# Turning the third to fifth pairs' q and k by the DMA crossbar instead of TensorE, with one more matmul on zeros

## The chip, the cores and the metric

The kernel runs on one core of a Trainium2 chip. The metric is the device time of one execution in microseconds, on an otherwise idle chip. "Half clock" and "full clock" below are TensorE's two rates. Pairs are counted from one: the "third pair" is `i == 2` in the code. The prediction counts from zero at places: its "pair 2" is the third pair here, its "pair 3" the fourth, its "pair 4" the fifth. A pair has nine units; in each, TensorE makes scores, ScalarE takes their exponential ("exp") and TensorE multiplies with the values. The "ring" is the line of transfers that SyncE has issued; GpSimd's transfers, w1 and w2 (the MLP's weights) among them, stand in another queue. The profile counts both on the same 16 DMA engines.

## The reference, cut to what matters

Block-sparse attention (a window, global blocks and sampled blocks of 32) over 4 batches of 8 heads, 768 positions, 64 wide, followed by a low-rank mixer and a two-layer MLP. Two heads make a pair; there are 16 pairs.

```python
scores = scale * np.matmul(q, k.transpose(0, 1, 3, 2))
scores = np.where(mask, scores, -1000000000.0)
attn = softmax(scores); out = np.matmul(attn, v)
x = out reshaped to (4, 768, 512)
u = x + (x^T @ U @ V)^T
result = u + relu(u @ w_ch1) @ w_ch2
```

(The last four lines are condensed.) q and k have a spread of 0.1, so scores are tiny.

## The kernel before

The scores need q and k with the head dimension on the partitions, so each pair is turned. The first four pairs run alone, before the MLP starts: they write q and k into the upper or lower 64 rows of tiles `qa` and `ka`, whose other 64 rows hold the mask as extra columns of the dot product. From the fifth pair (`HP` = 4) on the turned q and k stand in plain tiles `qT` and `kT`, and the mask is multiplied in by VectorE.

Before the change the second to fifth pairs are turned by TensorE into PSUM, and VectorE copies the result out. From the sixth on SyncE issues DMA transposes, SBUF to SBUF.

```python
def turn_dma(i, nm):
    st = sts.pop((i, nm))
    qkT[i, nm] = qkpool.tile([P, T, P], FP16, ...)
    keep(nc.sync.dma_start_transpose(out=qkT[i, nm], in_=st...))

def turn_part(i, nm, part):              # half a turn: 3 transposes
    ...
    turn_some(sts[i, nm], turning[nm], 3 * part, 3 * part + 3)
    if part == 1:
        ...
        if i < HP:
            for h in range(2):
                half_copy(nc.vector.tensor_copy, dst, h, pt, 0, T)
        else:
            keep(nc.vector.tensor_copy(out=qkT[i, nm], in_=pt))

def at_unit(i, u):                       # pair i, unit u of 9
    if (i, u) in MASKS:                  # (1, 8), (2, 8), (3, 8) among them
        mask_tiles(...)                  # two matmuls into PSUM, VectorE turns them into 0/1
    ...
    if u == 0 and i < 3:
        issue(i + 3)                     # SyncE: loads of q, k, v
    ...
    if (i, u) in WLOADS:                 # (1, 3), (1, 4), (2, 3), (2, 4): w1, by GpSimd
        WLOADS[i, u]()
    if u in (1, 2, 3, 4):
        turn_part(i + 1, "qk"[(u - 1) // 2], (u - 1) % 2)
    for _ in range({0: 1, 5: 2, 6: 1, 7: 1}.get(u, 0)):
        tails.popleft()()                # the mixer: at u = 6 and 7 the additions `xf`
    if u == 7: cast(i + 2, "q")          # GpSimd
    if u == 8: cast(i + 2, "k")
```

(Cuts at the dots.) The argument rests on VectorE's order. In the changed kernel's trace VectorE takes the copies and the additions `xf` in program order: the first addition, whose input was long there, starts only at 33.58 us, behind two copies that waited for a DMA until 32.82.

The softmax here doesn't subtract the row's maximum and nothing guards it: scores larger than these inputs give would overflow.

Of the kernel before, what the change touches and what calls it, by code (L numbers as in the profile page):

```python
# [21 lines left out]
def kernel(  # L22
# [12 lines left out]
    nc = tc.nc  # L35
# [6 lines left out]
    HP = H // 2  # L42
# [54 lines left out]
    keep = tc.keep_in_program_order  # L97
    flat = "p t n -> p (t n)"
# [10 lines left out]
    def pst_tile(shape, dtype, name, tag):  # L109
        n = singles[tag][0]  # L110
        singles[tag].rotate(1)
        return psp[tag].tile(shape, dtype, tag=f"{tag}{n}", name=name)
# [54 lines left out]
    def run_on(eng, us, ready=None):  # L167
        clk[eng] = max(clk[eng], (clk["pe"] if ready is None else ready) + LAG) + us
        return clk[eng]

    def mm(out, lhsT, rhs, start, stop, loose=False, us=0.0):
        clk["pe"] += us
        ins = nc.tensor.matmul(  # L173
            out, lhsT, rhs, start=start, stop=stop, skip_group_check=loose
        )
        keep(ins)
        return ins
# [16 lines left out]
    qa = [[consts.tile([P, S], FP16, name=f"qa{s}{h}") for h in range(2)] for s in range(2)]  # L194
    ka = [[consts.tile([P, S], FP16, name=f"ka{s}{h}") for h in range(2)] for s in range(2)]
# [15 lines left out]
    rows = [slice(0, D), slice(D, P)]  # L211
# [3 lines left out]
    lds, sts, qkT = {}, {}, {}  # L215
# [12 lines left out]
    def issue(i, names="qkv"):  # L228
        if i >= NPAIR:
            return  # L230
        for nm in names:
            keep(nc.sync.dma_start(out=new_ld(i, nm), in_=src_of(nm, i)))
# [30 lines left out]
    def turn_some(st, pt, t0, t1):  # L263
        for t in range(t0, t1):
            keep(
                nc.tensor.transpose(  # L266
                    out=pt[:, t, :],
                    in_=st[:, t].rearrange("p h d -> p (h d)"),
                    identity=id16,
                )  # L270
            )

    def turn_dma(i, nm):
        if i >= NPAIR:
            return
        st = sts.pop((i, nm))
        qkT[i, nm] = qkpool.tile([P, T, P], FP16, tag=nm + "T", name=nm + "T")
        keep(
            nc.sync.dma_start_transpose(
                out=qkT[i, nm], in_=st.rearrange("p t h d -> p (t h d)")  # L280
            )
        )
# [6 lines left out]
    for r in (slice(32, 64), rows[1]):  # L289
# [3 lines left out]
            out=id16, in_=zeros, pattern=[[-1, P]], compare_op=ALU.not_equal,  # L293
# [9 lines left out]
    def hot_rows(eng, st, h, n):  # L303
# [5 lines left out]
            out=sbi[0:NB].rearrange("z r w -> z (r w)"),  # L309
            in_=sampled_blocks.bitcast(I32),  # L310
# [28 lines left out]
    def warm_pe(n):  # L339
        for _ in range(n):  # L340
            mm(
                warm.rearrange("p (r n) -> p r n", r=4), zeros,
                zeros[:, None, :].broadcast_to([P, 4, P]), True, True,
            )
# [5 lines left out]
            out=eq[0:NB],  # L350
# [7 lines left out]
            out=cb[0:NB],  # L358
            in_=eq[0:NB].rearrange("z r c -> z c r"),
# [6 lines left out]
            out=cbd[0:NB, :, 0:NB],  # L366
# [16 lines left out]
    def mask_rows(eng, h, i, a, e):  # L383
        o = qa[0][h][mrows[h], a:e]
        if eng == "dve":
            keep(
                nc.vector.tensor_scalar(
                    out=o, in0=i[mrows[h]],
                    scalar1=-MASK_BIAS, scalar2=MASK_BIAS, op0=ALU.mult, op1=ALU.add,
                )  # L390
            )
        else:
            keep(
                nc.scalar.activation(
                    out=o, in_=i[mrows[h]],
                    func=AF.Copy, scale=-MASK_BIAS, bias=MASK_BIAS,
                )
            )
# [6 lines left out]
    cast0(nc.vector.tensor_copy, qst, qld, 0, TQ)  # L405
    mask_rows("dve", 0, pm0[:, 0, 0:QA], 0, QA)
    mask_rows("act", 1, pm1, 0, QA)
    pq = pst_tile([P, T, P], FP16, "pturn", tag="ps")
    pk = pst_tile([P, T, P], FP16, "pturn", tag="ps")
    turn_some(qst, pq, 0, TQ)  # L410
# [4 lines left out]
    def half_copy(eng, dst, h, pt, t0, t1):  # L415
        keep(
            eng(
                out=dst[h][rows[h], t0 * P : t1 * P],
                in_=pt[rows[h], t0:t1].rearrange(flat),
            )  # L420
        )
# [30 lines left out]
    def mask_tiles(g):  # L452

        pmk = [pst_tile([P, HS], FP32, "pmk", tag="ps") for c in range(2)]
        for c in range(2):
            mm(pmk[c], ka[0][c][mrows[c], g * P : (g + 1) * P],
               qa[0][c][mrows[c], c * HS : (c + 1) * HS], True, True)
        for c in range(2):
            keep(
                nc.vector.tensor_scalar(  # L460
                    out=m01[:, g, c * HS : (c + 1) * HS], in0=pmk[c],
                    scalar1=-1.0, scalar2=None, op0=ALU.is_ge,
                )
            )
# [470 lines left out]
    def turn_part(i, nm, part):  # L935

        if part == 0:
            turning[nm] = pst_tile([P, T, P], FP16, "pturn", tag="ps")
        turn_some(sts[i, nm], turning[nm], 3 * part, 3 * part + 3)
        if part == 1:  # L940
            del sts[i, nm]
            pt = turning.pop(nm)
            if i < HP:
                dst = {"q": qa, "k": ka}[nm][i % 2]
# [3 lines that stand above are left out]
                qkT[i, nm] = qkpool.tile([P, T, P], FP16, tag=nm + "T", name=nm + "T")  # L948
                keep(nc.vector.tensor_copy(out=qkT[i, nm], in_=pt))
            run_on("dve", 0.48)  # L950
# [25 lines left out]
    def cast_V():  # L976
        keep(
            nc.gpsimd.tensor_copy(
                out=Vt[0 : 2 * R, :, :],
                in_=mvld.rearrange("r (p t) -> r t p", t=T),  # L980
            )
        )

    def at_unit(i, u):
        if (i, u) in MASKS:
            mask_tiles(MASKS.index((i, u)))
        if i == 0:
            if u == 0:
                warm_pe(1)
                turn_some(qst, pq, TQ, T)  # L990
                turn_some(kst, pk, TK, T)
                for h in range(2):
                    mask_rows("dve", h, pm2[:, 0, 0:QB], QA, S)
                for nm, o, pt, t in (("q", qa[0], pq, TQ), ("k", ka[0], pk, TK)):
                    for h in range(2):
                        half_copy(nc.vector.tensor_copy, o, h, pt, t, T)
                for h in range(2):
                    keep(
                        nc.sync.dma_start(
                            out=qa[1][h][mrows[h], :], in_=qa[0][h][mrows[h], :]  # L1000
                        )
                    )
                issue(2, "q")
                keep(
                    nc.sync.dma_start(
                        out=uld, in_=moe_U.rearrange("(p t) r -> p (t r)", t=T)
                    )
                )
                issue(2, "k")
                for h in range(2):  # L1010
                    keep(nc.sync.dma_start(out=mvld[h * R : h * R + R], in_=moe_V))
                cast(1, "q")
                cast(1, "k")
                cast(1, "v")
            if u == 1:
                issue(2, "v")
            if u == 3:
                issue(3)
            if u == 6:
                cast(2, "q")  # L1020
                cast_U()
                cast(2, "k")
            if u == 4:
                turn_part(1, "q", 0)
                turn_part(1, "q", 1)
            if u == 6:
                turn_part(1, "k", 0)
                turn_part(1, "k", 1)
            return
        if u == 0 and i < 3:  # L1030
            issue(i + 3)
        if i == 1 and u == 2:
            cast_V()
            cast(2, "v")
        if i == 2 and u == 0:
            for h in range(2):
                keep(nc.sync.dma_start(out=Vd[rows[h]], in_=Vt[rows[0]]))
        if (i, u) in WLOADS:
            WLOADS[i, u]()
        if u in (1, 2, 3, 4):  # L1040
            turn_part(i + 1, "qk"[(u - 1) // 2], (u - 1) % 2)
        for _ in range({0: 1, 5: 2, 6: 1, 7: 1}.get(u, 0)):
            if tails:
                tails.popleft()()
        if u == 7:
            cast(i + 2, "q")
        if u == 8:
            cast(i + 2, "k")
        if u == 0 and i > 1:
            cast(i + 1, "v")  # L1050
# [211 lines left out]
```

## Time and profile before

| | before |
|---|---|
| median of the runs beside the changed kernel | 278.41 us (278.13 to 279.15, 4 runs) |
| profiled span | 277.7 us |
| TensorE, ScalarE, VectorE busy | 98%, 64%, 63% |
| chain of waits: TensorE | 92% |
| first exp of pairs 1 to 5 | 8.22, 17.36, 25.77, 34.28, 43.03 us |

These lines of the page cut the span into 40 slices of 6.9 us; each digit is an engine's busy share in tenths. The last line is the chain of waits by engine.

```profile
PE   7999999999999999999999999999999999999995
ACT  3799996786977957694864849584886201664000
DMA  6997965998969998997790999997100312000222
...
PE 92%; ACT 3%; DVE 2%; DMA 1%; POOL 0%; issue 0%; SPq 0%; DVEq 0%; POOLq 0%
```

TensorE hardly ever stops. In slices 2 to 6, most of the first four pairs, ScalarE (7, then 9s) and the DMA engines (9, 9, 7, 9, 6) are nearly full as well.

### The profile page before, as it was taken

What the parts mean: (1) busy time and instruction counts of PE and PEld (TensorE: products, weight loads), DVE (VectorE), ACT (ScalarE), POOL (GpSimd) and SP (SyncE); (2) the same over time, 40 slices, a digit from 0 to 9 for tenths busy, and PEclk for the clock granted to TensorE, in tenths of its full rate; (3) what the DMA queues carried; (4) which work ended last, traced back from release to release, by engine and by line L of the source; (5) the groups of instructions that cost most, each with busy time, mean ns of one, the idle gap of its engine ahead of it and who ended that gap; (6) DMA issues with size and microseconds to landing.
All of it is one profiled execution on the core that took longest, in us unless ns stands there. A gap on an engine that the chain in (4) does not pass through costs nothing.

```text
span 277.7 us, 8035 instructions
## 1 busy us (share of the span) xinstructions
PE 271.5 (98%) x3492; PEld 162.6 (59%) x3492; DVE 175.3 (63%) x286; ACT 177.0 (64%) x198; POOL 103.5 (37%) x137
## 2 busy tenths in 40 slices
PE   7999999999999999999999999999999999999995
PEld 2568775566656564756565564656565654655443
DVE  6767767888897987767756768776777451000112
ACT  3799996786977957694864849584886201664000
POOL 5659549506465736363603536361102020000000
PEclk9999999999999999999999999999999999999999
DMA  6997965998969998997790999997100312000222
GB/s 204 312 326 195 282 155 79 176 187 81 135 56 110 171 135 129 162 102 81 57 118 0 173 95 163 135 97 86 31 2 2 104 68 81 36 1 0 78 77 76
DMA packets 85484, 31.65 MB, mean 114 GB/s; under 512 B 75152, under 2 KB 83048, under 8 KB 85448
## 3 DMA queue, kind: packets, MB, share of 16 engines
q0 software_dynamic: 49824, 10.29, 43.4%
q1 hardware_dynamic: 35268, 20.62, 34.3%
q8 instruction: 27, 0.44, 0.7%
q10 hardware_dynamic: 356, 0.22, 0.3%
q14 instruction: 9, 0.07, 0.1%
HBM read 27.84 MB, written 6.29 MB: 123 GB/s over the span
## 4 chain that ended last, share of the span: by engine, by line
PE 92%; ACT 3%; DVE 2%; DMA 1%; POOL 0%; issue 0%; SPq 0%; DVEq 0%; POOLq 0%
PE pch L173 30%; PE pt L173 30%; PE psc L173 13%; PE pav L173 13%; ACT est L498 3%; PE pa L173 2%; DMA qld<-in_q_dram 1%; PE pturn L266 1%; PE ph L173 1%; POOL xh L598 0%; PE warm L173 0%; PE puT L711 0%; DVE xh L541 0%; PE pmk L173 0%; DVE xs L589 0%
## 5 line engine op out<-in xcount | busy, mean ns | idle before, releaser
L498 ACT ACTIVATE est<-psc 128x1024 f16<-128x1024 f32 x144 | 142.9, 1028 | 46.1 <-PE psc L173 44.7
L173 PE MATMUL pt<-uT,w1t 64*128 64x384 f16 (+1 forms) x896 | 94.4, 324 | 0.0
L173 PE MATMUL pch<-w2t,tT 64*128 64x512 f16 (+3 forms) x688 | 93.6, 372 | 0.1
L519 DVE TENSOR_TENSOR est<-est,m 128x1024 f16<-128x1024 f16 x108 | 78.3, 740 | 18.2 <-ACT est L498 16.8
L173 PEld LDWEIGHTS <-w1t 64*128 64x128 f16 (+1 forms) x896 | 46.0, 95 | 36.2 <-PE pt L173 8.3
L173 PEld LDWEIGHTS <-tT 64*128 64x128 f16 (+1 forms) x688 | 38.2, 95 | 36.9 <-PE pch L173 1.6
L736 ACT ACTIVATE tT<-pt 128x768 f16<-128x768 f32 (+1 forms) x48 | 36.6, 772 | 26.0 <-PE pt L173 26.0
L173 PEld LDWEIGHTS <-est 128*128 128x128 f16 x1152 | 41.4, 97 | 10.9 <-issue 5.0
L173 PE MATMUL pav<-vt,est 128*128 128x65 f16 x1152 | 44.5, 193 | 0.1
L791 DVE TENSOR_TENSOR of<-xf,pch 128x1024 f32<-128x1024 f32 (+3 forms) x16 | 15.2, 951 | 42.7 <-PE pch L173 42.7
L173 PE MATMUL psc<-qT,kT 64*128 64x512 f16 (+1 forms) x288 | 40.6, 323 | 0.3 <-ACT est L498 0.3
L598 POOL CAST xh<-xs 128x768 f16<-128x768 f32 x12 | 10.5, 872 | 79.6 <-DVE xs L589 74.0
L684 POOL CAST uh<-xf 128x768 f16<-128x768 f32 x12 | 13.9, 1162 | 26.1 <-DVE xf L675 14.5
L173 PE MATMUL psc<-qa,ka 128*128 128x512 f16 (+1 forms) x96 | 22.0, 333 | 0.6 <-ACT est L498 0.5
L738 DVE TENSOR_SCALAR tT<-pt 128x768 f16<-128x768 f32 (+1 forms) x20 | 18.3, 917 | 5.9 <-PE pt L173 5.8
L173 PEld LDWEIGHTS <-kT 64*128 64x128 f16 x288 | 14.6, 94 | 12.5 <-issue 0.7
L261 POOL DMA_DIRECT2D vt<-in_v_dram x20 | 16.4, 822 | 3.4 <-DMA w2t<-in_moe_w_ch_dram 3.4
L261 POOL DMA_DIRECT2D qst<-in_q_dram x20 | 16.3, 821 | 0.1
L261 POOL DMA_DIRECT2D kst<-in_k_dram x20 | 16.3, 822 | 0.0
L589 DVE TENSOR_TENSOR xs<-pav,rcp 128x768 f32<-128x768 f32 x12 | 11.5, 958 | 1.2
L675 DVE TENSOR_TENSOR xf<-xs,ph 128x768 f32<-128x768 f32 x12 | 11.4, 951 | 1.2 <-PE ph L173 1.2
L173 PEld LDWEIGHTS <-ka 128*128 128x128 f16 (+1 forms) x108 | 9.0, 99 | 3.7 <-issue 1.8
(70 smaller groups left out, 132.2 us busy)
## 6 DMA issues: line engine op xcount, KB each, us to landing
out_dram<-of SPq DMA_DIRECT2D x9, 512.0 KB, 3.3
vld<-in_v_dram SPq DMA_DIRECT2D x6, 384.0 KB, 6.5
w1t<-in_moe_w_ch_dram POOLq DMA_DIRECT2D x4, 512.0 KB, 9.1
w2t<-in_moe_w_ch_dram POOLq DMA_DIRECT2D x4, 512.0 KB, 10.1
qld<-in_q_dram SPq DMA_DIRECT2D x5, 384.0 KB, 5.5
kld<-in_k_dram SPq DMA_DIRECT2D x5, 384.0 KB, 6.8
qst<-in_q_dram POOLq DMA_DIRECT2D x20, 96.0 KB, 4.1
kst<-in_k_dram POOLq DMA_DIRECT2D x20, 96.0 KB, 4.4
```

The source lines that it names most:

```text
L173: ins = nc.tensor.matmul(out, lhsT, rhs, start=start, stop=stop, skip_group_check=loose)
L261: keep(nc.gpsimd.dma_start(out=o[:, h], in_=src_of(nm, i)[:, h]))
L266: nc.tensor.transpose(out=pt[:, t, :], in_=st[:, t].rearrange("p h d -> p (h d)"), identity=id16,)
L498: keep(nc.scalar.activation(out=est, in_=psc, func=AF.Exp, scale=0.125))
L519: keep(nc.vector.tensor_tensor(out=o, in0=o, in1=m, op=ALU.mult))
L589: nc.vector.tensor_tensor(out=xs.rearrange("p (c j) (h d) -> p c (j h) d", c=2, h=2), in0=pv[:, :, :, 0:D], in1=rcp[:, :, :, None].broadca ...
L598: keep(nc.gpsimd.tensor_copy(out=xh, in_=xs))
L675: nc.vector.tensor_tensor(out=u.rearrange("p (c j) n -> p c j n", c=2), in0=xs.rearrange("p (c j) n -> p c j n", c=2), in1=ph[:, :, 0:HS]. ...
L684: keep(nc.gpsimd.tensor_copy(out=uh, in_=u))
L736: keep(nc.scalar.activation(out=o, in_=i, func=AF.Relu))
L738: keep(nc.vector.tensor_scalar_max(out=o, in0=i, scalar1=0.0))
L791: nc.vector.tensor_add(out=of, in0=xfs[b][:, sc : sc + nsc, n0:n1], in1=pch)
```

## The change

The intent is to take 36 transposes off TensorE, the engine that carries the chain, and to put them on the DMA crossbar. The third and fourth pairs still need their rows inside `qa` and `ka`, so VectorE copies them there, SBUF to SBUF. The fifth pair's tiles are filled straight by the crossbar. One more matmul on zeros at the start is to keep TensorE busy while it waits for q.

```diff
     mask_rows("act", 1, pm1, 0, QA)
+    warm_pe(1)
     pq = pst_tile([P, T, P], FP16, "pturn", tag="ps")
...
-        if u in (1, 2, 3, 4):
-            turn_part(i + 1, "qk"[(u - 1) // 2], (u - 1) % 2)
+        if u == 0:
+            turn_dma(i + 1, "q")
+            turn_dma(i + 1, "k")
+        if u in (6, 7) and i + 1 < HP:
+            nm = "qk"[u - 6]
+            for h in range(2):
+                keep(
+                    nc.vector.tensor_copy(
+                        out={"q": qa, "k": ka}[nm][(i + 1) % 2][h][rows[h], :],
+                        in_=qkT[i + 1, nm][rows[h]].rearrange(flat),
+                    )
+                )
```

## The prediction

> **What bounds the kernel now.** I read the page's chain of waits first (TensorE 92% of it), then the slices, and then split the run at the point where its character changes. About 50 to 278 us TensorE works without a gap (tenths of busy all 9). Each engine's instruction order for that stretch, compared between the two kernels, is the same apart from the turns. So only the first four pairs (8 to 43 us) are in play. The stretches of that part:
>
> ```profile
> core 0: us, PE busy (x) PEld busy (x) DVE busy (x) ACT busy (x) POOL busy (x), PEclk, DMA share, GB/s
> 9.90:19.50 9.60, 9.29 (x125) 6.54 (x124) 6.67 (x15) 9.58 (x11) 4.48 (x7) 1.00 1.08 297
> 19.50:29.00 9.50, 9.44 (x142) 7.16 (x141) 7.57 (x17) 9.49 (x11) 8.21 (x13) 1.00 0.84 221
> 29.00:38.50 9.50, 9.47 (x146) 7.25 (x144) 6.73 (x16) 9.49 (x11) 5.55 (x10) 1.00 1.06 273
> ```
>
> TensorE and ScalarE are both full, and the DMA engines are as well. The chain of waits in order of time says which of the two leads:
>
> ```profile
> 18.11 0.24 PE pav L173 x8
> 18.35 0.17 PE pturn L266 x3
> 18.51 0.52 PE psc L173 x4
> 19.04 0.24 PE pav L173 x8
> 19.28 0.17 PE pturn L266 x3
> ```
>
> Here TensorE leads, and a half turn (three transposes) costs 0.17 us on the path. But ScalarE is close behind. Successive exps start 0.904 to 0.926 us apart when nothing holds them, and 0.94 to 1.04 us apart where TensorE was late. Pair 2's nine exps span 8.52 us (25.77 to 34.28), against 9 x 0.913 = 8.21 us at ScalarE's own pace. That leaves only 0.3 us a pair to gain, however much TensorE is relieved.
>
> Then the issue order around the point where the new transposes go:
>
> ```profile
> 22.15 0.82 POOL L241 CAST vt<-vld 128x768 f16<-128x768 f32 x1
> 22.92 1.11 POOL L438 DMA_DIRECT2D w1t<-in_moe_w_ch_dram  x2
> 22.99 0.37 SPq L232 DMA_DIRECT2D vld<-in_v_dram  x1
> ...
> 24.80 0.34 PE L173 MATMUL pmk<-qa,ka 64*128 64x384 f16 x2
> ...
> 25.06 0.60 PE L173 MATMUL psc<-qa,ka 128*128 128x512 f16 x2
> ```
>
> SyncE's load of pair 4's v waits for GpSimd's cast of pair 2's v, which frees the buffer. It goes out only at 22.99. The next pair's first scores are at 25.06. In SyncE's order of the changed kernel the two new transposes stand behind that load. What a transpose takes today:
>
> ```profile
> w1t<-in_moe_w_ch_dram POOLq DMA_DIRECT2D x4, 512.0 KB, 9.1
> qT<-qst SPq DMA_TRANSPOSE x11, 4.8
> kT<-kst SPq DMA_TRANSPOSE x11, 4.4
> ```
>
> The last figure is us from issue to landing. For qT it is 2.8 at the least and 7.6 at the most; for kT 2.8 and 8.8. Each holds SyncE's queue about 1.2 us.
>
> **What the Trainium skill says.** "VectorE: DVE Perf Modes", section "The three transpose paths", gives 1309 ns for a 128x128 block through the DMA crossbar and 390 ns on TensorE. In this trace six blocks take 0.34 us of TensorE's path and at least 2.8 us by DMA, so the DMA way is off the engines but late. "DMA: Bandwidth & Descriptors", section "Queues, rings and completion order", says each DMA engine goes round-robin between queues, packet by packet. The trace agrees. The first kT, sent while a w2 load ran on GpSimd's queue, had no packet for 3.1 us, moved its 768 packets of 256 B in 5.1 us about one for one with the other queue's, and landed after 8 us; alone, the same packets take 1.1 us. "TensorE: Matmul & The Clock Gate", section "Part 1: The HAM clock gate", says that the array falls to half clock after an idle window of about 3.4 us and comes back after a busy one. The trace shows the start: 128x512 matmuls begin 0.427 us apart until about 9.5 us, then 0.216 us apart. "VectorE: DVE Perf Modes", section "Rules for kernel authors", gives copies of 16-bit data inside SBUF up to four times the rate. The 768-column SBUF copy took 0.34 us here, the same width out of PSUM 0.56 us.
>
> **The change part by part.**
> - TensorE loses 3 pairs x 12 transposes: 12 halves x 0.17 = 2.0 us of work. Only some 0.3 us a pair can come through, and what pair 1 wins is swallowed by the wait below. I count 0.6 us.
> - VectorE loses 8 copies of 0.56 and 2 of 0.55 us, and gains 8 of about 0.34 us: 2.9 us less work, none of it on the path.
> - The extra matmul on zeros fills a hole at 4.6 to 5.4 us in which TensorE waits for q. It costs nothing, and if it makes TensorE busy enough to reach full clock one window sooner, the start gains up to about 1 us (TensorE is on the chain from 5.4 to 9.9). The phase of that window is not in my hands; I count 0.3 us.
> - SyncE gains six transposes. Pair 2's go out at about 23.4 and 24.7 us. GpSimd's first w1 load (two DMAs, 1 MB in 256 packets of 4096 B, 324 ns each, 16 per engine) runs from 25.1 to 30.3 us. The v load's packets run from 24.0 to 25.6 and stand ahead in the same ring. So qT's packets (48 per engine) meet the w1 load and share one for one: 16 of them go while w1 lasts, the other 32 after. My estimate is qT landed at 31 to 31.5 and kT at 32 us.
> - VectorE executes in order. Its two qa copies stand ahead of the first xf addition, and its two ka copies ahead of the second. The mask-tile matmuls at the end of the pair (24.80 in the trace) need the PSUM tiles that those additions read. The first can go when qT + 0.68 + 0.56 is past, the second when kT + 0.68 + 0.56 is past: 32 + 1.3 = 33.3 us instead of 25.0. **TensorE stands about 8.4 us**, and ScalarE with it.
> - After such an idle stretch TensorE restarts at half clock. At 4 us of half clock, and scores and values filling the time, about 2.0 us are lost.
> - Pair 3's transposes go out behind pair 5's three loads and the Vd copies, some 4.5 us after the restart, and would land about 8.5 us after it. VectorE wants them about 8 us after it, and TensorE would stop only about 9.7 us after. The second w1 load starts about then. I count 0.7 us, mostly the chance that they meet. Pair 4's are wanted only nine units later, straight from the crossbar, and cost nothing.
>
> Sum: +8.4 + 2.0 + 0.7 - 0.6 - 0.3 = +10.2 us on 278.2, that is 288.4 us. I put it at 287.8, because each of the landing times is taken near the late end of what the contention allows.
>
> **The rivals.**
> 1. The transposes slip in before w1. Then qT lands 2.8 us after 23.4 and kT 2.8 after 24.7, at 27.5. TensorE would wait until 28.8, 3.8 us, without half the clock penalty; with about 1.5 us gained elsewhere the time would be about 281. For it: qT's issue ends at 24.6, before w1's first packet. Against it: the v load is ahead in the same ring, and the kT that met w2 started late and slowly.
> 2. No wait at all, the relief counts: 0.9 us from the pairs and up to 1 us at the start, 276.5. Against it: even the least landing time is past the first need at 25 us, and VectorE's order lets nothing around it.
> 3. Both w1 loads collide with transposes: a second stop of 4 to 6 us when pair 3's kT meets the second load, plus a second restart at half clock, about 294. Against it: after the first stop that load is issued later than the transposes. For it: the margins are 1 us.
>
> **Range and chances.** The main branch gives 284 to 291, depending on where in w1's burst the landing falls (1 us of landing is 1 us of time). Rival 1 has about 15%, rival 3 about 10%, rival 2 under 3%. I set 282.5 to 292.5. Slower by over 2% means over 283.7 us: 0.86. Within 2%: 0.12. Faster by over 2% would need 5.6 us, more than the parts hold: 0.02.
>
> **What would show it.** In the profile of the changed kernel: VectorE idle before the first qa copy from qT for several us, released by a DMA; a hole in TensorE and ScalarE from about 25 to 33 us; after it 128x512 matmuls 0.427 us apart for some us; the landing times of pair 2's qT and kT beyond 6 us; the stretch from 50 us on of the old length and only moved. I would be wrong if kT lands before 28 us, if the copies stand elsewhere in VectorE's executed order, or if the first matmuls reach full clock so early that the start alone gives back over 2 us.

## The result, and the profile after

The changed kernel took 299.63 us (median of four runs, 293.59 to 302.73) against 278.41. Ratios here are the mean time of one kernel's fast runs over that of the other's of the same rounds, so not quite the ratio of the medians. By that ratio it is 1.061 (95% interval 1.049 to 1.073). Two of the four runs, the profiled one of 301.89 among them, count as slow because they lie over 1.5% above the fastest; the ratio rests on the other two, 293.59 and 297.38. A second set of six runs (last experiment below) gave 302.34 us and a ratio of 1.089, with a profile that shows the same picture.

The slices of the changed kernel, now 7.5 us each, and its chain:

```profile
PE   8990391899999999999999999999999999999996
ACT  4991081495969778577768384858487700466000
PEclk9996597599999999999999999999999999999999
DMA  6999499239999699999969199999630123100122
...
PE 78%; DMA 11%; POOL 3%; DVE 3%; SPq 2%; ACT 1%; issue 1%; POOLq 0%; DVEq 0%; ACTq 0%
```

There are two holes, in slices 4 to 5 and in slice 7. TensorE and ScalarE stop together, and TensorE's granted clock falls with them. DMA now has 11% of the chain. The stretches that hold the holes, with each engine's busy us:

```profile
core 0: us, PE busy (x) PEld busy (x) DVE busy (x) ACT busy (x) POOL busy (x), PEclk, DMA share, GB/s
19.50:29.00 9.50, 3.45 (x56) 2.76 (x54) 0.29 (x1) 4.41 (x5) 3.45 (x5) 0.79 1.06 287
29.00:38.50 9.50, 3.37 (x20) 1.77 (x20) 4.00 (x9) 1.02 (x1) 3.38 (x5) 0.50 0.54 67
38.50:48.00 9.50, 6.63 (x98) 4.96 (x97) 3.23 (x9) 7.46 (x8) 2.02 (x4) 0.99 1.09 239
48.00:58.00 10.00, 4.90 (x34) 2.92 (x34) 3.59 (x9) 2.05 (x2) 3.33 (x5) 0.54 0.55 87
```

From 19.5 to 29 us only the DMA engines are full; from about 24 us on every other engine stands. The first hole, from the timeline (start, duration, engine, and in brackets the idle time before and what ended it; rows are left out at the dots):

```profile
21.83 1.12 POOL L439 DMA_DIRECT2D w1t<-in_moe_w_ch_dram  x2
21.90 0.37 SPq L232 DMA_DIRECT2D vld<-in_v_dram  x1
...
22.32 1.55 SPq L279 DMA_TRANSPOSE qT<-qst  x1
...
23.93 4.61 SPq L279 DMA_TRANSPOSE kT<-kst  x1
32.82 0.72 DVE L1048 COPY qa<-qT 64x768 f16<-64x768 f16 x2 [12.07 <-DMA qT<-qst]
...
34.18 0.47 PE L173 MATMUL pmk<-qa,ka 64*128 64x384 f16 x1 [11.15 <-DVE xf L646]
...
35.61 0.47 PE L173 MATMUL pmk<-qa,ka 64*128 64x384 f16 x1 [0.95 <-DVE xf L646]
...
36.01 1.04 PE L173 MATMUL psc<-qa,ka 128*128 128x512 f16 x2
```

This is a chain of four links. SyncE sends qT at 22.32. VectorE gets it at 32.82, having stood 12 us. TensorE's mask-tile matmul stands 11 us for an addition that is queued behind VectorE's copy. When TensorE comes back, two score matmuls take 1.04 us instead of 0.60, which is half clock.

The trace's packet records say why qT needs over 10 us. Until about 26 us the ring still moves plain loads; qT's first packet is at 26.5. The w1 load's 256 packets of 4096 B run from 24 to 31 us, and from 27 to 30 us the transpose moves 134 packets of 256 B against 121 of w1's, about one for one. It has 768 to move. Once w1 is through, the rest go in some 2 us.

The second hole, into the fourth pair, has the same links, with kT as the late one:

```profile
40.04 1.42 SPq L279 DMA_TRANSPOSE qT<-qst  x1
...
41.15 1.07 POOL L439 DMA_DIRECT2D w1t<-in_moe_w_ch_dram  x2
...
41.50 1.55 SPq L279 DMA_TRANSPOSE kT<-kst  x1
...
52.06 0.72 DVE L1048 COPY ka<-kT 64x768 f16<-64x768 f16 x2 [4.05 <-DMA kT<-kst]
...
53.83 1.03 PE L173 MATMUL psc<-qa,ka 128*128 128x512 f16 x2
```

GpSimd issues the second w1 load between qT and kT. Its packets run from 44.4 to 51.1 us, kT's from 45.3 to 51.6.

The start of each pair's first exp sums this up:

| start of first exp, us | pair 1 | pair 2 | pair 3 | pair 4 | pair 5 | last matmul |
|---|---|---|---|---|---|---|
| before | 8.22 | 17.36 | 25.77 | 34.28 | 43.03 | 274.73 |
| changed | 6.79 | 15.42 | 37.15 | 54.96 | 65.25 | 296.96 |
| difference | -1.4 | -1.9 | +11.4 | +20.7 | +22.2 | +22.2 |

The whole loss is made before the fifth pair and carried to the end unchanged.

### The profile page after: what moved, and what is told of

It is laid out like the page before. It is cut to its first block, busy times and chain, and to the rows that moved or that the text cites.

```text
span 300.1 us, 7973 instructions
## 1 busy us (share of the span) xinstructions
PE 274.0 (91%) x3457; PEld 162.2 (54%) x3457; DVE 172.9 (58%) x284; ACT 177.3 (59%) x198; POOL 103.3 (34%) x137
## 4 chain that ended last, share of the span: by engine, by line
PE 78%; DMA 11%; POOL 3%; DVE 3%; SPq 2%; ACT 1%; issue 1%; POOLq 0%; DVEq 0%; ACTq 0%
PE pch L173 28%; PE pt L173 27%; PE pav L173 10%; PE psc L173 9%; DMA kT<-kst 4%; DMA qT<-qst 3%; DMA kld<-in_k_dram 3%; PE pa L173 2%; ACT est L499 1%; DMA qld<-in_q_dram 1%; PE ph L173 1%; POOL kst L247 1%; POOL vt L241 1%; POOL Vt L979 1%; SPq L279 0%
## 5 line engine op out<-in xcount | busy, mean ns | idle before, releaser
L520 DVE TENSOR_TENSOR est<-est,m 128x1024 f16<-128x1024 f16 x108 | 78.3, 740 | 18.2 <-ACT est L499 16.8
L173 PEld LDWEIGHTS <-w1t 64*128 64x128 f16 (+1 forms) x896 | 46.0, 95 | 36.2 <-PE pt L173 8.3
L173 PEld LDWEIGHTS <-est 128*128 128x128 f16 x1152 | 42.5, 98 | 12.2 <-issue 7.6
L173 PE MATMUL pav<-vt,est 128*128 128x65 f16 x1152 | 45.3, 195 | 0.0
L173 PE MATMUL psc<-qa,ka 128*128 128x512 f16 (+1 forms) x96 | 24.2, 355 | 1.2 <-ACT est L499 0.7
L173 PE MATMUL pmk<-qa,ka 64*128 64x384 f16 x12 | 3.5, 366 | 19.7 <-DVE xf L646 19.7
L660 POOL CAST uh<-xf 128x384 f16<-128x384 f32 x6 | 3.1, 517 | 26.4 <-DVE xf L646 26.4
```

The source lines that it names most:

```text
L173: ins = nc.tensor.matmul(out, lhsT, rhs, start=start, stop=stop, skip_group_check=loose)
L520: keep(nc.vector.tensor_tensor(out=o, in0=o, in1=m, op=ALU.mult))
L660: keep(nc.gpsimd.tensor_copy(out=uh3, in_=u3))
```

## The experiments

For each run, the table gives the gaps into the third, fourth and fifth pairs: from the start of a pair's last exp to the start of the next pair's first exp, in the run's profile (0.99 us is normal, 0.90 into the fifth pair). Times are medians of all runs of a set.

| run | gap into 3rd, 4th, 5th pair, us | time, us | before beside it, us | ratio |
|---|---|---|---|---|
| before | 0.99, 0.99, 0.90 | | | |
| changed | 14.2, 9.5, 0.90 | 299.63 | 278.41 | 1.061 |
| e1 matmul only | 1.0, 1.0, 0.90 | 278.51 | 278.23 | 1.000 |
| e2 fifth pair only | 1.0, 1.0, 3.77 | 280.65 | 278.23 | 1.008 |
| e3 all w1 later | 8.3, 2.7, 17.0 | 305.16 | 278.23 | 1.093 |
| e4 turn first | 3.0, 5.0, 0.90 | 283.96 | 278.23 | 1.021 |
| e5 no turn | 0.99, 0.99, 0.90 | 278.41 | 278.57 | 0.9995 |
| e6 zeros in the holes | 12.0, 13.2, 0.90 | 303.83 | 278.57 | 1.089 |
| e7 copies late | 11.6, 4.7, 0.90 | 295.52 | 278.57 | 1.062 |
| e8 clear road | 4.7, 5.5, 0.90 | 289.44 | 278.57 | 1.039 |
| e9 clear road, early copies | 4.0, 1.6, 0.90 | 284.3 | 278.56 | 1.018 |
| e10 second w1 later | 12.8, 2.9, 0.90 | 293.9 | 278.56 | 1.056 |
| e11 changed again | 14.7, 13.0, 0.90 | 302.34 | 278.56 | 1.089 |

(e3, e6 and e9 each had one slow run and the changed kernel's first set two; the medians have them in, the ratios do not.)

**e1, the matmul on zeros alone.**

```diff
     mask_rows("act", 1, pm1, 0, QA)
+    warm_pe(1)
```

> The kernel before plus the one matmul on zeros, nothing else. Theory A (the extra matmul lets TensorE reach full clock one window sooner, as the changed kernel's profile shows from 4.6 us on, and the first exp starts 1.4 us earlier): 276.8 us, 1.0 to 1.4 us faster than before, first exp near 6.8 us. Rival B (the early clock in that profile was the chance phase of the window, not the matmul): 278.2 us, same as before within 0.2 us, and half clock until about 9 us.

The ratio is 0.9997 (0.9971 to 1.0024): no gain that this resolves. In the profile the first exp starts at 7.45 us instead of 8.22, and the clock record has full clock from 6.9 us instead of 9.5. The other profiles with this matmul go the same way (full clock at 3.8 to 6.8 us where there is a record, first exp at 6.79 to 7.58). But the kernel before has one profile only, of a run of 279.56 us, over 1 us above its median, so the matmul and the chance phase cannot be told apart from it. Both kernels' runs spread over about 1 us (before: 278.02 to 279.36), and the time shows no gain. Rival B holds for the time; its half clock until 9 us is not what the profile shows.

**e2, only the fifth pair by DMA.**

```diff
-        if u in (1, 2, 3, 4):
+        if u == 0 and i == HP - 1:
+            turn_dma(i + 1, "q")
+            turn_dma(i + 1, "k")
+        if u in (1, 2, 3, 4) and i < HP - 1:
             turn_part(...)
```

> Only the fifth pair is turned by DMA (straight into its qT and kT, no VectorE copies), third and fourth stay on TensorE, with the extra matmul. Theory A (the damage is all in the third and fourth pairs, whose transposes are wanted at once; the fifth's are wanted nine units later): as the run with the matmul alone, minus 0 to 0.4 us, about 276.5, no VectorE wait for a DMA before the 45th us. Rival B (any crossbar transpose in this stage hurts, because it meets the w1 load): 2 to 8 us slower than the run with the matmul alone.

It was 0.8% slower than the kernel before (1.0083, 1.0016 to 1.0149): two runs at 279.0 us, two over 282. In the profile (of a 282.9 us run) the fifth pair's transposes go out at 33.3 and 36.2 us into the second w1 load, which runs to 39.0, with plain loads still ahead in the ring. qT's first packet is at 37.5, kT's last at 42.4, and TensorE's scores wait 2.7 us for it. Theory A's time fails. Against e1 (278.51) the median is 2.1 us slower, the low edge of B's range, and two of the four runs are 0.5 us slower only. So nine units of slack are not always enough; whether w1 or the plain loads cost more here, this run does not say.

**e3, all w1 loads later.**

```diff
-            ((1, 3), (1, 4), (2, 3), (2, 4), (HP, 0), ...
+            ((2, 8), (3, 0), (3, 1), (3, 2), (HP, 0), ...
```

> The changed kernel with all four w1 loads issued after the fourth pair's transposes. Theory A (the landing is late mainly because the 256-byte packets share the DMA engines one for one with w1's 4096-byte packets): the third pair's kT lands at 27 to 28 us instead of 33.4, the first hole shrinks from about 13 us to 5 to 6, the second from about 8 us to under 2; 283 to 287 us in all, w1 now perhaps 1 to 2 us late for the stage after. Rival B (the transposes are late because they are issued late and stand behind the plain loads in the same ring; w1 matters little): first hole 11 us or more, 292 us or more.

Where w1 was taken away, theory A's landing came true: the third pair's kT had its last packet at 27.4 us (33.0 in the changed kernel), and the fourth's gap fell to 2.7. The first gap was 8.3 rather than A's 5 to 6. But w1 now met the fifth pair's transposes, and the total missed A by 18 us. From this run's waits (total us, times, longest):

```profile
PE psc L173 <- DMA kT<-kst: 15.9, 1, 15.9
```

TensorE stood 15.9 us for one kT, beside which over 2 MB of w1 went by. Moving the load moves the hole. That is strong evidence for the contention; the total is the worst of all runs.

**e4, the transposes ahead of the loads in SyncE's order.**

```diff
+        if u == 0:
+            turn_dma(i + 1, "q")
+            turn_dma(i + 1, "k")
         if u == 0 and i < 3:
             issue(i + 3)
...
-        if u == 0:
-            turn_dma(i + 1, "q")
-            turn_dma(i + 1, "k")
```

> The changed kernel with the two transposes of each pair put ahead of the pair's three loads in SyncE's order; the same transfers, the same VectorE copies. Theory A (lateness of issue is what costs: the load of v ahead of them waits for GpSimd's cast): the third pair's transposes go out at about 16 to 18 us and land before 23, no hole there; the fourth's go out at about 25 us, land by 31 and are wanted at about 31, hole 0 to 1 us; 276 to 278 us in all. Rival B (contention with w1 and the loads decides, not the place in the order): the fourth pair's kT still lands at the end of w1's burst or after, a hole of 4 us or more; 282 us or more. Rival C (VectorE's copies in order are the cost by themselves): as B but with no DMA named before the copies.

One reordering of the same work takes 16 us of the 21 back. The third pair's transposes go out at 16.8 and 18.7 us and end at 22.7 and 23.5, still behind the backlog of loads, a gap of 3.0. The fourth's meet w1 (kT ends at 36.3), a gap of 5.0. So A has the third pair's issue about right but not its landing, and B has the fourth pair's gap (4 us or more) and the total (283.96, B said 282 or more). Place in the order and contention both count: e9 keeps this order, takes w1 away, and has 1.6 for the 5.0.

**e5, no turn at all for the third and fourth pairs.** This is the bound. Its output is wrong, which doesn't matter for the time. The comparison with the reference did not notice, because the scores are so small that the old q and k give nearly the same attention.

```diff
-        if u in (1, 2, 3, 4):
+        if u in (1, 2, 3, 4) and i == HP - 1:
             turn_part(...)
```

> Wrong results on purpose: the kernel before with the extra matmul, and the third and fourth pairs' q and k not turned and not copied at all (their scores use what the first and second pairs left). It bounds what any other way of turning these two pairs could give back. Theory A (ScalarE is so close behind that only about 0.3 us a pair comes through): 0.4 to 0.8 us faster than the run with the matmul alone, some 277.8 us. Rival B (the turns cost what TensorE's chain shows, 0.69 us a pair, or more, because VectorE is relieved too): 1.4 us faster or more, under 277.1 us.

The ratio is 0.9995 (0.9982 to 1.0007, 14 runs), and the median is 0.1 us below that of the run with the matmul alone. Both theories were too high: there is nothing to be had. During the third pair, with the fourth's 12 transposes gone, nine exps span 8.445 us against 8.518 in e1, so 0.07 us came through. During the second pair TensorE ran ahead only to meet the next limit; the chain of this run in order of time (start, us, what):

```profile
8.32 8.50 DMA qld<-in_q_dram
...
16.96 0.83 POOL qst L247
...
18.93 0.82 POOL kst L247
...
20.66 1.51 POOL Vt L979
```

A load, then GpSimd's casts, carry the chain where TensorE's transposes did. The bound holds for the third and fourth pairs with the loads where they are; leaving out the fifth pair's turn, or bringing the loads earlier too, was not tried.

**e6, matmuls on zeros in the holes.**

```diff
+        if u == 8 and i in (1, 2):
+            idle = (the next score tile)
+            for _ in range({1: 48, 2: 32}[i]):
+                mm(idle[:, 0, :]..., zeros, ..., True, True)
         if (i, u) in MASKS:
             mask_tiles(...)
```

> The changed kernel with 48 and 32 matmuls on zeros (10.4 and 6.9 us at full clock) where TensorE would stand at the end of the second and third pairs. Theory A (after each hole TensorE comes back at half clock, which costs 1.0 and 1.7 us by the spacing of the first exps in the changed kernel's profile): the first exps after the holes come 0.9 to 1.0 us apart instead of 1.8, no 128x512 score matmul 0.43 us apart after 10 us, and about 2 to 3 us less than the changed kernel at equal holes, if the zeros end before the data is there. Rival B (the slow restart is from waits of VectorE and GpSimd, not from the clock): the same spacing of exps as without the zeros.

Theory A holds where the zeros reached to the end of the hole. The timeline after the first one:

```profile
23.73 10.52 PE L173 MATMUL idle<-m 128*128 128x512 f16 x48
34.82 0.60 PE L173 MATMUL psc<-qa,ka 128*128 128x512 f16 x2
35.84 0.59 PE L173 MATMUL psc<-qa,ka 128*128 128x512 f16 x2
```

Score matmuls take 0.60 us, not 1.04, and the first two exps come 1.01 us apart instead of 1.83. In the second hole the zeros ended some 3 us early, and the restart was at half clock again (1.76 us). The total was not better, at 303.83 (302.29 for the fast runs): the fourth pair's transposes met the second w1 load, and the second gap was 13.2 (9.5 and 13.0 in the changed kernel's two profiles). So A's spacing is shown and its saving in the total is not. By the spacing of the exps the restarts of these runs cost 0.7 to 1.7 us each; the holes themselves outweigh that.

**e7, the copies behind the mask tiles.**

```diff
-        if u in (6, 7) and i + 1 < HP:       # q's copies at 6, k's at 7
+        if u == 8 and i + 1 < HP:            # all four
```

> The changed kernel with the four copies of a pair moved behind the mask tiles of the pair's last unit in VectorE's order; everything else as it is. Theory A (the landing of kT sets the end of the hole; the copies' place costs only the 1.3 us of work that stands between landing and first scores): holes as long within 1 to 1.5 us, 1 to 3 us less in all, 291 to 300 us. Rival C (VectorE's order is the cause: the blocked additions, masks and GpSimd's casts behind them delay the next loads and transposes): 287 us or less.

It took 295.52 us, inside A's range. The first gap is 11.6 instead of 14.2. The second is 4.7, because GpSimd and SyncE were no longer held up and the fourth pair's transposes (last packet at 38.3 us) were through before w1. So A's second hole is missed and C's mechanism is worth 5 to 8 us there, but C's total is not reached, and it falls as the main cause. In the total the gain is not clear: 295.52 is 7 us under the changed kernel's second set, but no better than the two fast runs of its first (293.59 and 297.38).

**e8, a clear road.** e4's order, e3's w1 places, e7's late copies, and the fifth pair on TensorE (shown against the changed kernel).

```diff
         for n, at in enumerate(
-            ((1, 3), (1, 4), (2, 3), (2, 4), (HP, 0), ...
+            ((2, 8), (3, 0), (3, 1), (3, 2), (HP, 0), ...
+        if u == 0 and i < HP - 1:           # ahead of the loads
+            turn_dma(i + 1, "q")
+            turn_dma(i + 1, "k")
+        if u in (1, 2, 3, 4) and i == HP - 1:
+            turn_part(i + 1, "qk"[(u - 1) // 2], (u - 1) % 2)
-        if u == 0:                          # behind them
-            turn_dma(i + 1, "q")
-            turn_dma(i + 1, "k")
-        if u in (6, 7) and i + 1 < HP:      # two copies in each
+        if u == 8 and i + 1 < HP:           # all four
```

> Third and fourth pairs by DMA with a clear road: their transposes ahead of the loads in SyncE's order, the copies behind the mask tiles, all w1 loads after the fourth pair's transposes, the fifth pair turned by TensorE so that no transpose meets w1. Theory A (it is only lateness, from w1's packets and from the place in the order): the third pair's kT lands by 24, the fourth's by 29 to 31, both before they are wanted; no hole over 0.5 us; as the run without turns or 0.3 us more, 277.5 to 278.3 us, if w1 comes in time for the next stage (at about 46 us; if not, 1 to 2 us more). Rival B (256-byte transposes in this stage slow the loads themselves so that the casts come late): holes of 2 us or more at GpSimd's casts, 281 us or more.

The transposes behaved as A said: last packets of the third pair at 23.5 us, of the fourth at 30.0. The time did not: 289.44 us, with gaps of 4.7 and 5.5. The timeline at the third pair shows what I had not thought of:

```profile
25.59 0.83 POOL L247 CAST kst<-kld 128x768 f16<-128x768 f32 x1
25.71 1.81 DVE L1050 COPY qa<-qT 64x768 f16<-64x768 f16 x2
26.36 0.95 POOL L241 CAST vt<-vld 128x768 f16<-128x768 f32 x1
...
27.96 1.03 PE L173 MATMUL psc<-qa,ka 128*128 128x512 f16 x2 [3.22 <-DVE ka L1050]
```

Two copies that take 0.35 us each alone take 1.81 together beside GpSimd's casts, and TensorE, after standing 3.2 us, comes back at half clock. At 0.35 us each TensorE would still have stood some 2.1 us (an estimate: 3.22 less 1.09), so the copies' place behind the mask tiles costs more than their slowness. At the fourth pair one copy beside GpSimd's casts and DMA issues took 1.93 us.

**e9, the clear road with the copies where the change has them.** As e8, with the copies at units 6 and 7.

```diff
-        if u == 8 and i + 1 < HP:           # all four
+        if u in (6, 7) and i + 1 < HP:      # two copies in each
```

> The clear road again (transposes ahead of the loads, all w1 loads behind the fourth pair's turn, fifth pair on TensorE), but with the copies where the change has them, in the pair's seventh and eighth units, where GpSimd casts nothing. Theory A (what was left in the run with late copies, some 4.2 us of hole a pair and a restart at half clock, came from the copies: 0.88 to 1.93 us each beside GpSimd's casts against 0.35 alone, all on the path of the first scores): qa copies about 0.35 us each; a hole of 1.5 to 2.5 us at the third pair (kT lands at 24, wanted at 21 to 23), none over 0.5 us at the fourth; 279.5 to 281.5 us. Rival B (the DMA way costs holes whatever the place of the copies, because the casts and loads shift): 286 us or more.

284.3 us, outside A's range and below B's. The qa copies take 0.34 to 0.36 us each, as A said, and the fourth pair's gap is 1.6. The third pair's is 4.0, more than A allowed: its kT ends at 23.5 us behind the loads' backlog, and the copies that should run at 21 run at 23.3 and 24.6. A restart at half clock follows (exps 1.86 us apart). In the total the clear road is no better than e4 (283.96), which still had w1 in the way of the fourth pair: there the third pair's gap was 3.0, with no restart at half clock.

**e10, only the second half of w1 later.**

```diff
-            ((1, 3), (1, 4), (2, 3), (2, 4), (HP, 0), ...
+            ((1, 3), (1, 4), (3, 1), (3, 2), (HP, 0), ...
```

> The changed kernel with only the second pair of w1 loads moved behind the fifth pair's transposes; the first pair stays where it meets the third pair's turn. Theory A (the second hole, 8.6 us in the changed kernel's profile, is the fourth pair's kT meeting the second w1 load; my prediction left this out): first hole as before, 11 to 13 us; second hole under 3 us; 287 to 292 us, and less spread than 294 to 303. Rival B (the second hole comes from pair 5's loads ahead in the ring): second hole 5 us or more, as the changed kernel.

The second gap is 2.9 (9.5 and 13.0 in the two profiles of the changed kernel) and the first 12.8, as before. Of this run's waits for transposes, one line is left for `qa` and none for `ka`:

```profile
DVE qa L1048 <- DMA qT<-qst: 11.6, 2, 10.5
```

Beside it in the same rounds the changed kernel (e11) took 302.34, so the move is worth 8.4 us. The time, 293.9, is 1.9 above A's range although both holes are of the size that A gave: its sum was short (the fifth pair's first exp is 13.8 us later than before). The six runs lie within 3 us of one another. So most of the second hole is the meeting with the second w1 load, and the sixth pair's loads ahead in the ring (the theories' "pair 5", still there) are not its cause.

**e11, the changed kernel again**, with no edit.

> The changed kernel itself again, for its spread and beside these runs. Theory A (its time depends on whether the fourth pair's kT gets in before the second w1 load): 293 to 303 us again, in two clusters some 6 us apart, and the profile's second hole long or short with the time. Rival B (the spread was the chip's slower state): all runs within 1% of one another.

302.34 us, with four runs at 301.9 to 302.6 and two at 306.2 and 306.3. It is in two clusters, 4 us apart rather than 6, and higher than the first set. Neither expectation held: 306 is outside A's range, and the spread of 1.5% is over B's 1%. Its profile, of a 306.2 us run, has the same waits as the first profile:

```profile
DVE qa L1048 <- DMA qT<-qst: 13.6, 2, 12.4
DVE ka L1048 <- DMA kT<-kst: 9.5, 1, 9.5
```

The second line is the fourth pair's kT, 13 us on the way beside the second w1 load. So this set's spread is not the chip's slower state: all its runs count as fast. I have no profile of a short run. That the 293.59 us run was one in which the fourth pair's kT got in before w1 fits e10's 293.9, but is argued, not shown.

## Why the prediction was right or wrong

The direction and the mechanism of the first stop were right. The size was not: 287.8 with a range to 292.5, against 299.63. In the profile the fifth pair starts 22.2 us late, 12 more than the sum of +10.2: the second stop and its restart make up 9.5 of these 12 (8.6 + 1.6 measured, 0.7 counted).

- **First stop, predicted 8.4 us.** The links are as written (VectorE's order, the additions, the mask-tile matmuls). The size was off: the gap is 14.2 us, 13.2 more than normal. Of that, 1.8 us is that the change brought TensorE to the waiting place earlier, so 11.4 stand against the 8.4. Mis-sized terms: the loads' backlog reached to 26 us and w1 to 31, so qT reached VectorE at 32.8 instead of 31 to 31.5, and kT landed at 33.5 instead of 32, with its copies from 34.05. e3 shows the part due to w1: without it the gap is 8.3.
- **Half clock, predicted 2.0 us.** Right in kind, by e6. After the first hole the exps show 0.8 us lost (1.83 us apart instead of 1.03), after the second 1.6 (1.93, 1.29 and 1.23 instead of 1.03, 0.92 and 0.90). So the 2.0 for the one restart counted was too much; the second restart was not counted.
- **"I count 0.7 us, mostly the chance that they meet" is the step that failed.** The fourth pair's kT met the second w1 load in both profiles of the changed kernel, and the second gap was 9.5 and 13.0 us, 8.5 to 12 us over normal. The prediction had the fourth pair's turn landed 8.5 us after the restart and wanted after 9.7; from the restart at 36.0 us, qT reached VectorE 10.7 us later and kT 16. That is rival 3, to which I gave 10%, and its stop of 4 to 6 us was still too short. e10 shows that without the meeting the extra is 2 us. The reasoning placed two events of about 1 us apart on either side of each other and then weighed the good side nine to one; a margin that small is no better than even.
- **Gains, predicted 0.6 and 0.3 us.** Measured bound: nothing (e5, ratio 0.9995; e1, 0.9997). TensorE's 0.17 us a half turn stands on the chain of waits, yet removing it gave 0.07 us in a pair. At the start the changed kernel was 1.4 us ahead at the first exp and 1.9 at the second pair's, more than counted, and the first stop took it all. (The hole that the extra matmul fills is 4.8 to 5.4 us in the timeline, not 4.6 to 5.4.) The chain names who came last, not how far behind the next one is.
- **VectorE's copies of "about 0.34 us"** were right in the changed kernel where GpSimd was quiet (0.35), and 0.57 beside a cast, as with one ka copy at 34.4 us. e8 shows how far this can go.
- **The later part "only moved"** was right: +22.2 us at the fifth pair and +22.2 at the last matmul. "Pair 4's ... cost nothing" (the transposes of the fifth pair as counted here) was right in the changed kernel, where the gap stays 0.90: w1 was through at 51.1 us and these transposes go out at 54.7. e2 and e3 show it at 2.9 and 16 us over normal.

No version of this change beat the kernel before. With e5's bound at zero for the third and fourth pairs, there was next to nothing to win by turning these two elsewhere.

## What to carry to other kernels

Before moving work off the leading engine, test what its removal alone is worth: a kernel that leaves the work out, with wrong results, gave the answer here (nothing) for the price of one run. Moving work onto DMA queues that are already full turns a cost of a few hundred nanoseconds in order into a landing that depends on everything else in flight, and here the small packets lost most beside the large ones (134 of 256 B moved for 121 of 4096 B). When two transfers are due within a microsecond of each other, count the collision at even odds with its full price, and look at which in-order engine stands behind the late one.

## What the Trainium skill lacked or had wrong

- "Advanced Engine Details and Errata", section "X-Bar Transpose (TRN2)", says that transposes are as fast as regular DMAs, 350 to 400 GB/s. Not here: in the trace of the kernel before, a transpose of 196,608 B moved as 768 packets of 256 B in 1.11 us with nothing beside it (177 GB/s), and two in a row in e7 took 1.66 us (237 GB/s), while plain loads in the former trace moved up to 376 KB a us.
- "DMA: Bandwidth & Descriptors", section "Queues, rings and completion order", gives the round-robin, but not what it does to unequal packets: 134 packets of 256 B against 121 of 4096 B in 3 us, so the transpose got about a fifteenth of the bytes. It also lacks that a transfer issued while the other queue is busy can start late: in the trace of the kernel before, qT at 57.5 us had nothing of its own ring ahead and took 4.0 us from issue to first packet, against 1.2 to 1.3 us alone; but uT at 70.8 us, also beside the other queue, took 1.2.
- "SBUF — State Buffer", section "SBUF: two separate sides", has the lock between VectorE and GpSimd; e8 agrees, with copies of 0.88 to 1.93 us against 0.35. "VectorE: DVE Perf Modes", section "Rules for kernel authors", recommends such copies for their rate without that caution beside it.
- "TensorE: Matmul & The Clock Gate", section "Part 1: The HAM clock gate", gives an idle window of about 3.4 us. Here less was enough: in e8 the clock record falls to half at 26.6 us, 1.8 us after TensorE's last matmul, and in e9 at 25.8 us, where by the trace TensorE had no gap over 1.1 us and was busy 1.7 of the last 3.4 us. The section also speaks of short idle times that do it, without a number. What no page gives is the price of one such restart in a chain that another engine shares: 0.7 to 1.7 us by the exps here.
